# Statistics one tile ahead, a down product in two pieces and other room for two pools, in a four-layer forward and backward kernel

## Chip, cores, metric

One core of a Trainium2 chip. The metric is the device time of one execution in microseconds (us), as the median of several executions. TensorE is called PE, VectorE DVE, ScalarE ACT, GpSimd POOL; SyncE (SP) issues most of the transfers.

## The reference

Four residual layers, A, B, A, B, on x of 2048 x 512 in bf16, then the gradients for x and five weights. `setup_inputs` draws everything from a normal distribution times 0.05.

```python
def _A_ref(x, wqkv, wo):                    # linear attention, 32 heads of 16
    q, k, v = ...                           # (x @ wqkv) by heads
    phi = lambda t: jnp.where(t > 0, t + 1, jnp.exp(t)) + 1e-6
    pq, pk = phi(q), phi(k)
    kv = einsum("bhsd,bhse->bhde", pk, v);  z = einsum("bhsd->bhd", pk)
    num = einsum("bhqd,bhde->bhqe", pq, kv)
    den = einsum("bhqd,bhd->bhq", pq, z)[..., None] + 1e-6
    return (num / den).reshape(B, S, D) @ wo

def _B_ref(x, w_gate, w_up, w_down):        # GLU, 512 -> 1376 -> 512
    h = sigmoid(x @ w_gate) * (x @ w_up)
    return h @ w_down

x = x + _A_ref(_layernorm(x), A_wqkv, A_wo)
x = x + _B_ref(_layernorm(x), B_w_gate, B_w_up, B_w_down)
x = x + _A_ref(_layernorm(x), A_wqkv, A_wo)
x = x + _B_ref(_layernorm(x), B_w_gate, B_w_up, B_w_down)
# reference(): the value and its vjp with grad_out
```

## The kernel before, where the change touches it

The 2048 rows are 16 tiles of 128 (`NST`), four tiles make a block (`NB`), the 1376 hidden columns are 11 chunks (`NFC`). `after(k, x, y)` only fixes that x stands behind y; the compiler orders everything else by itself. First, the norm of layer 0: statistics on DVE, the inverse root of the variance on POOL, the scaling on DVE, then transposes on PE.

```python
if l == 0:
    src, rstd = narrow(k, st), k.rstd[l][:, st:st + 1]
    stats = k.small.tile([P, 6], F32, name="ln_stats")
    bn = nc.vector.bn_stats(stats[:], src)
    if 1 < st < 6:
        after(k, bn, self.applied[1 if st == 2 else st - 3])
    mv = k.small.tile([P, 2], F32, name="ln_mv")
    nc.vector.bn_aggr(mv[:], stats[:])
    mean = mv[:, 0:1]
    add = nc.gpsimd.tensor_scalar(rstd, mv[:, 1:2], EPS_LN, None, ALU.add)
    if 0 < st < 6:
        after(k, add, self.power)
    self.power = nc.gpsimd.tensor_tensor(rstd, rstd, k.neghalf[:, 0:1], ALU.pow)
    self.applied.append(nc.vector.tensor_scalar(self.h[b][:, j, :], src, mean, rstd, ALU.subtract, ALU.mult))
    # ... then four transposes on PE into T_ps
```

Between these stand the keys of the same tile: `k_ps` on PE, the exponential on ACT, two steps on DVE that end in `pk_t`, and then on PE the sum `E_ps` of h and pk.

```python
    nc.scalar.activation(pk, k_ps[:], ACT.Exp)
    nc.vector.tensor_scalar(pk, pk, 1.0, EPS, ALU.min, ALU.add)
    self.pks.append((pk, nc.vector.scalar_tensor_tensor(pk, k_ps[:], 1.0 + EPS, pk, ALU.add, ALU.max)))
```

Second, the first GLU. One chunk is eight matmuls (`g_ps`, `u_ps`), a tanh and a copy or two on ACT, one or two steps on DVE. The down product of a block is 44 matmuls, and it is issued at the start of the next block.

```python
def down(b):
    ys = [k.bank([P, D], F32, name="y_ps") for _ in range(NB)]
    for fcs in (range(NFC - 1), (NFC - 1,)):
        for j in range(NB):
            for fc in fcs:
                nc.tensor.matmul(ys[j][:], lhsT=hhs[b][fc][:, rows(j)], rhs=k.wd[:, fc, :], ...)
    for j in range(NB):
        add_x(k, b * NB + j, ys[j])

for b in range(NBLK):
    hhs[b] = []
    if b:
        down(b - 1)
    for fc in range(NFC):
        hh, sd = glu(k, ln.hT[b], fc, fc % 2 == 1, b == fc == 0)
        hhs[b].append(hh)
        # ... stores, and the next layer's norms
```

Third, the backward of that GLU, the inner gradient stage. Its two pools lie on the left side of SBUF, where the attention backward, which runs before and after it, has its own. At its end the attention backward wants `dqT_t` and `qn_l`, and a filling job (`Fill`, matmuls of another layer that plug PE's gaps) wants `hf_t`; all three are issued by SP, in order.

```python
def b_bwd(k, l):
    p_g = ctx.enter_context(k.tc.tile_pool(name=f"bb_g{l}", bufs=2))      # dhh_t
    p_dd = ctx.enter_context(k.tc.tile_pool(name=f"bb_dd{l}", bufs=5))    # dd_t
```

## Time and profile before

| | before |
|---|---|
| median of 4 executions (lowest to highest) | 1097.89 us (1096.7 to 1098.25) |
| span of the profiled one | 1095.3 us |
| PE busy | 1055.7 us, 96% |
| DVE, ACT, POOL busy | 51, 41, 28% |

First what DVE waited for most in the first 32 us (total us, times, longest us),

```profile
DVE h_t L295 <- POOL rstd L294: 4.5, 10, 0.9
```

then its timeline (start us, us busy, and in brackets the idle time before and what ended it),

```profile
7.81 0.17 DVE L289 BATCH_NORM_AGGREGATE ln_mv<-ln_stats 128x2 f32<-128x6 f32 x1
7.89 0.66 DVE L285 BATCH_NORM_STATS2 ln_stats<-x 128x6 f32<-128x512 bf16 x1
8.97 0.41 DVE L295 TENSOR_SCALAR h_t<-x,ln_mv,rstd 128x512 bf16<-128x512 bf16 x1 [0.42 <-POOL rstd L294]
```

and POOL's timeline for the same tile:

```profile
8.07 0.22 POOL L291 TENSOR_SCALAR rstd<-ln_mv 128x1 f32<-128x1 f32 x1 [1.81 <-DVE ln_mv L289]
8.37 0.57 POOL L294 TENSOR_TENSOR rstd<-rstd,neghalf 128x1 f32<-128x1 f32 x1
```

The aggregate starts at 7.81, POOL's add at 8.07, its power at 8.37, the scaling at 8.97: the round trip takes 1.16 us from the start of the aggregate.

### The profile page before, as it was taken

What the parts mean: (1) busy time and instruction counts of PE and PEld (TensorE: products, weight loads), DVE (VectorE), ACT (ScalarE), POOL (GpSimd) and SP (SyncE); (2) the same over time, 40 slices, a digit from 0 to 9 for tenths busy, and PEclk for the clock granted to TensorE, in tenths of its full rate; (3) what the DMA queues carried; (4) which work ended last, traced back from release to release, by engine and by line L of the source; (5) the groups of instructions that cost most, each with busy time, mean ns of one, the idle gap of its engine ahead of it and who ended that gap; (6) DMA issues with size and microseconds to landing.
All of it is one profiled execution on the core that took longest, in us unless ns stands there. A gap on an engine that the chain in (4) does not pass through costs nothing.

```text
span 1095.3 us, 15173 instructions
## 1 busy us (share of the span) xinstructions
PE 1055.7 (96%) x5355; PEld 493.4 (45%) x5448; DVE 554.0 (51%) x1029; ACT 444.0 (41%) x930; POOL 303.1 (28%) x410
## 2 busy tenths in 40 slices
PE   6989899999999999999999999998999999999998
PEld 3444344444444444444444444443444444465443
DVE  7686865669845454435776534557867200001110
ACT  4476766547845555543324533334326100000010
POOL 5333523203742525141622200003613200011110
PEclk9999999999999999999999999999999999999999
DMA  9997978789999989999997788769989998599991
GB/s 264 273 238 245 286 208 235 212 201 220 289 239 229 255 185 277 191 225 210 335 349 201 206 278 242 224 180 273 304 233 349 266 227 191 124 216 226 245 250 35
DMA packets 401869, 258.50 MB, mean 236 GB/s; under 512 B 308720, under 2 KB 371472, under 8 KB 400512
## 3 DMA queue, kind: packets, MB, share of 16 engines
q1 hardware_dynamic: 386608, 208.12, 77.9%
q0 software_dynamic: 15184, 49.39, 13.5%
q8 instruction: 43, 0.70, 0.3%
q14 instruction: 34, 0.28, 0.1%
HBM read 76.19 MB, written 106.79 MB: 167 GB/s over the span
## 4 chain that ended last, share of the span: by engine, by line
PE 66%; DMA 3%; DVE 2%; ACT 1%; issue 1%; POOL 1%; SPq 0%; ACTq 0%; DVEq 0%; POOLq 0%
PE dw_ps L1280 19%; PE dh_ps L840 7%; PE dh_ps L934 7%; PE dhh_ps L196 6%; PE dh_ps L1119 4%; PE y_ps L196 4%; PE dw_ps L1298 3%; PE g_ps L196 3%; PE u_ps L196 3%; PE dh_ps L1110 2%; PE fill_ps L250 2%; PE CT_ps L1038 2%; PE dq_ps L196 2%; PE dpk_ps L196 1%; DMA hf_t<-sv_hhT 1%
## 5 line engine op out<-in xcount | busy, mean ns | idle before, releaser
L1280 PE MATMUL dw_ps<-set_t,rows_t 128*128 128x512 bf16 (+1 forms) x1008 | 203.6, 362 | 0.8
L1280 PEld LDWEIGHTS <-rows_t 128*128 128x128 bf16 x1024 | 100.1, 98 | 103.7
L666 POOL TENSOR_TENSOR sd_t<-sd_t,hh_t 128x512 bf16<-128x512 bf16 x68 | 80.9, 1189 | 150.2 <-DVE hh_t L661 84.7
L1199 DVE CAST dw_new<-dw_ps 128x512 bf16<-128x512 f32 (+1 forms) x20 | 12.4, 654 | 184.1 <-PE dw_ps L1280 160.9
L1199 ACT CAST dw_new<-dw_ps 128x512 bf16<-128x512 f32 (+1 forms) x20 | 10.5, 561 | 225.7 <-PE dw_ps L1280 188.1
L904 ACT ACTIVATE t_sb<-dh_ps,rstd 128x512 f32<-128x512 f32 x64 | 43.5, 680 | 134.3 <-PE dh_ps L840 75.8
L196 PE MATMUL g_ps<-hT_t,wg 128*128 128x512 bf16 (+1 forms) x360 | 90.8, 375 | 1.2 <-DVE sd_t L663 0.6
L196 PE MATMUL u_ps<-hT_t,wu 128*128 128x512 bf16 (+1 forms) x360 | 90.7, 375 | 0.5 <-DVE hh_t L661 0.2
L196 PE MATMUL dhh_ps<-gT_t,wdT 128*128 128x512 bf16 x342 | 89.0, 379 | 1.2 <-ACT dhh_t L961 1.0
L934 PE MATMUL dh_ps<-wgT,dd_t 128*128 128x512 bf16 x174 | 66.0, 379 | 0.4
L934 PE MATMUL dh_ps<-wuT,dd_t 128*128 128x512 bf16 x169 | 64.1, 379 | 0.1
L661 DVE SCALAR_TENSOR_TENSOR hh_t<-sd_t,u_ps 128x512 bf16<-128x512 bf16 x88 | 59.4, 680 | 6.3 <-ACT sd_t L660 5.4
L1200 POOL DMA_DIRECT2D out_dram<-dw_new x36 | 19.3, 541 | 153.6 <-DVE dw_new L1199 150.2
L660 ACT ACTIVATE sd_t<-g_ps,onef 128x512 bf16<-128x512 f32 x88 | 60.5, 695 | 2.5
L963 DVE TENSOR_TENSOR dd_t<-dhh_t,sh_t 128x1024 bf16<-128x1024 bf16 x44 | 30.0, 691 | 58.9 <-ACT dhh_t L961 58.6
L659 ACT ACTIVATE g_ps<-g_ps 128x512 f32<-128x512 f32 x88 | 52.8, 606 | 7.7 <-PE g_ps L196 7.3
L749 DVE TENSOR_TENSOR sd_t<-dhh_t,sd_t 128x1024 bf16<-128x1024 bf16 x44 | 30.4, 691 | 48.7 <-POOL sd_t L666 45.8
L196 PEld LDWEIGHTS <-wu 128*128 128x128 bf16 x360 | 35.2, 98 | 41.5 <-issue 0.7
L196 PEld LDWEIGHTS <-wdT 128*128 128x128 bf16 x352 | 34.4, 98 | 42.6 <-issue 1.5
L196 PEld LDWEIGHTS <-wg 128*128 128x128 bf16 x360 | 34.5, 98 | 41.4 <-issue 1.8
L840 PEld LDWEIGHTS <-sd_t 128*128 128x128 bf16 x352 | 34.5, 98 | 41.5
L934 PEld LDWEIGHTS <-dd_t 128*128 128x128 bf16 x352 | 34.4, 98 | 41.6
(166 smaller groups left out, 1832.1 us busy)
## 6 DMA issues: line engine op xcount, KB each, us to landing
sv_sd<-sd_t SPq DMA_DIRECT2D x22, 512.0 KB, 3.7
sv_ddT<-dd_t SPq DMA_DIRECT2D x40, 256.0 KB, 5.0
sv_h<-h_t POOLq DMA_DIRECT2D x16, 512.0 KB, 5.3
sv_qr<-pe_t POOLq DMA_DIRECT2D x16, 512.0 KB, 4.9
sh_t<-sv_sd SPq DMA_DIRECT2D x8, 1024.0 KB, 6.8
rows_t<-sv_h SPq DMA_DIRECT2D x16, 512.0 KB, 8.5
sv_ddN<-nat_t SPq DMA_DIRECT2D x15, 512.0 KB, 4.4
set_t<-sv_ddN SPq DMA_DIRECT2D x12, 512.0 KB, 6.6
```

Source lines behind the costliest of these rows:

```text
L196: i = k.nc.tensor.matmul(out, lhsT=lhs(c), rhs=rhs(c), start=(c == 0), stop=(c == n - 1))
L659: nc.scalar.activation(g_ps[:], g_ps[:], ACT.Tanh, scale=-0.5)
L660: nc.scalar.activation(sd[:, 0, :], g_ps[:], ACT.Identity, bias=k.onef[:], scale=-1.0)
L661: nc.vector.scalar_tensor_tensor(hh[:], sd[:, 0, :], 0.5, u_ps[:], ALU.mult, ALU.mult)
L666: nc.gpsimd.tensor_tensor(sd[:, 1, :], sd[:, 1, :], hh[:], ALU.mult)
L749: k.last_mul = nc.vector.tensor_tensor(dd, dhh[:].unsqueeze(1).to_broadcast([P, 2, SB]), dd, ALU.mult)
L840: k.nc.tensor.matmul(dh[j][:], lhsT=dds[fc][:, a, rows(j)], rhs=(k.wuT, k.wgT)[a][:, fc, :], start=(a == fc == 0), stop=(a == 1 and fc == ...
L904: nc.scalar.activation(t_sb[:], dh_ps, ACT.Identity, scale=rstd, accum_out=c1[:])
L934: nc.tensor.matmul(acc[b][j][:], lhsT=dd[:, a, rows(j)], rhs=(k.wuT, k.wgT)[a][:, fc, :], start=(fc == 0 and a == 0), stop=(fc == NFC - 1 ...
L1119: nc.tensor.matmul(dh[j][:], lhsT=lhs(j, c), rhs=rhs(c), start=False, stop=stop and c == NDC - 1)
L1280: k.nc.tensor.matmul(ps[ic][:, 0:w], lhsT=h_m[:, ic * P:(ic + 1) * P], rhs=t_m, start=(m == 0), stop=(m == n - 1))
L1298: k.nc.tensor.matmul(p[0:r, :], lhsT=t[:, f:f + r], rhs=g_t, start=(i == 0 and st == 0), stop=(i == len(srcs) - 1 and st == NST - 1))
```

## The change

Three parts. The intent of the first is to take POOL's round trip off DVE's path by computing the statistics of tile t+1 before tile t is scaled. The second gives ACT and DVE two chunks of the GLU to work on while PE does the other half of the down product. The third keeps the inner gradient's tiles clear of the attention backward's room, so that its first loads need not wait.

```diff
         if l == 0:
-            (statistics, add, power and scaling of tile st, as above)
+            if st == 0:
+                self.stats(0)
+            if st + 1 < NST:
+                self.stats(st + 1)
+            mean, rstd = self.got.pop(st)
+            self.applied.append(nc.vector.tensor_scalar(self.h[b][:, j, :], narrow(k, st), mean, rstd, ALU.subtract, ALU.mult))
...
+    def stats(self, st):
+        bn = nc.vector.bn_stats(stats[:], narrow(k, st))
+        if 1 < st < 6:
+            after(k, bn, self.applied[st - 2])
+        (aggregate, add and power as above, without the order between tiles on POOL)
...
-    def down(b):
-        ys = [k.bank([P, D], F32, name="y_ps") for _ in range(NB)]
+    def down(b, js):
+        ys = {j: k.bank([P, D], F32, name="y_ps") for j in js}
         (and range(NB) becomes js in its loops)
...
         if b:
-            down(b - 1)
+            down(b - 1, range(2))
         for fc in range(NFC):
             hh, sd = glu(k, ln.hT[b], fc, fc % 2 == 1, b == fc == 0)
             hhs[b].append(hh)
+            if b and fc == 1:
+                down(b - 1, range(2, NB))
...
-    down(NBLK - 1)
+    down(NBLK - 1, range(NB))
...
-        p_g = ctx.enter_context(k.tc.tile_pool(name=f"bb_g{l}", bufs=2))
-        p_dd = ctx.enter_context(k.tc.tile_pool(name=f"bb_dd{l}", bufs=5))
+        p_g = ctx.enter_context(k.tc.tile_pool(name=f"bb_g{l}", bufs=2, side="right"))
+        p_dd = ctx.enter_context(k.tc.tile_pool(name=f"bb_dd{l}", bufs=5, side="right"))
```

More of the change, by code (lines that the diff above doesn't have):

```diff
@@ L267, in __init__ @@
         self.k, self.l = k, l
-        self.h, self.hT, self.done, self.applied = {}, {}, 0, []
+        self.h, self.hT, self.done, self.got, self.applied = {}, {}, 0, {}, []
     def need(self, st):
@@ L282, in one @@
         if l == 0:
-            src, rstd = narrow(k, st), k.rstd[l][:, st:st + 1]
-            stats = k.small.tile([P, 6], F32, name="ln_stats")
-            bn = nc.vector.bn_stats(stats[:], src)
-            if 1 < st < 6:
-                after(k, bn, self.applied[1 if st == 2 else st - 3])
-            mv = k.small.tile([P, 2], F32, name="ln_mv")
-            nc.vector.bn_aggr(mv[:], stats[:])
-            mean = mv[:, 0:1]
-            add = nc.gpsimd.tensor_scalar(rstd, mv[:, 1:2], EPS_LN, None, ALU.add)
-            if 0 < st < 6:
-                after(k, add, self.power)
-            self.power = nc.gpsimd.tensor_tensor(rstd, rstd, k.neghalf[:, 0:1], ALU.pow)
-            self.applied.append(nc.vector.tensor_scalar(self.h[b][:, j, :], src, mean, rstd, ALU.subtract, ALU.mult))
+            if st == 0:
[4 more added lines that the diff above has]
+            self.applied.append(nc.vector.tensor_scalar(self.h[b][:, j, :], narrow(k, st), mean, rstd, ALU.subtract, ALU.mult))
             if j % 2 == 0:
@@ L326, in one @@
                 store_turned(k, k.sv[l]["hT"][b], self.hT[b])
+    def stats(self, st):
+        k, nc = self.k, self.k.nc
+        rstd = k.rstd[self.l][:, st:st + 1]
+        stats = k.small.tile([P, 6], F32, name="ln_stats")
+        bn = nc.vector.bn_stats(stats[:], narrow(k, st))
+        if 1 < st < 6:
+            after(k, bn, self.applied[st - 2])
+        mv = k.small.tile([P, 2], F32, name="ln_mv")
+        nc.vector.bn_aggr(mv[:], stats[:])
+        nc.gpsimd.tensor_scalar(rstd, mv[:, 1:2], EPS_LN, None, ALU.add)
+        nc.gpsimd.tensor_tensor(rstd, rstd, k.neghalf[:, 0:1], ALU.pow)
+        self.got[st] = mv[:, 0:1], rstd
     def turn(self, j):
@@ L685, in store @@
             nc.sync.dma_start(out=sv["sd"][:, n - 1:n + 1], in_=sd[:].rearrange("p n a s -> p n (a s)"))
-    def down(b):
-        ys = [k.bank([P, D], F32, name="y_ps") for _ in range(NB)]
+    def down(b, js):
+        ys = {j: k.bank([P, D], F32, name="y_ps") for j in js}
         for fcs in (range(NFC - 1), (NFC - 1,)):
-            for j in range(NB):
+            for j in js:
                 for fc in fcs:
@@ L693, in down @@
                                      start=(fc == 0), stop=(fc == NFC - 1))
-        for j in range(NB):
+        for j in js:
             add_x(k, b * NB + j, ys[j])
```

## The prediction

> **What bounds the kernel now.** I read the page first. TensorE (PE) is busy 96% of the 1095.3 us span and every slice's granted clock is full, so only PE idle time, 1095.3 - 1055.7 = 39.6 us, can be won without removing matmuls, and the change removes none. Then I read what PE waited for, longest first. The columns are total us, times, longest us.
>
> ```profile
> PE 1055.7 (96%) x5355; PEld 493.4 (45%) x5448; DVE 554.0 (51%) x1029; ACT 444.0 (41%) x930; POOL 303.1 (28%) x410
> ...
> PE T_ps L299 <- DVE h_t L295: 6.6, 2, 5.9
> PE y_ps L692 <- DVE hh_t L661: 3.0, 2, 2.2
> PE fill_ps L250 <- DMA hf_t<-sv_hhT: 2.6, 1, 2.6
> ...
> PE T_ps L299 <- DVE pk_t L470: 1.9, 1, 1.9
> ...
> PE dhh_ps L196 <- ACT dhh_t L961: 1.0, 2, 0.6
> ```
>
> The changed places are the first norm (T_ps), the down product of the first GLU (y_ps L692), and the two ends of the inner gradient stage (dhh_ps, and fill_ps just after it). Third, busy time by stretch. After the stretch come its length and the busy us of PE, PE loads, DVE, ACT, POOL.
>
> ```profile
> 5.87:10.20 4.33, 3.50 (x16) 1.64 (x16) 3.41 (x9) 1.70 (x4) 1.72 (x5) 1.00 0.97 301
> 10.20:14.00 3.80, 1.92 (x9) 0.85 (x9) 3.07 (x10) 1.54 (x3) 3.46 (x9) 1.00 0.85 246
> ...
> 106.10:131.00 24.90, 23.69 (x137) 10.50 (x137) 21.13 (x40) 20.30 (x46) 10.16 (x14) 1.00 0.78 242
> 131.00:142.80 11.80, 9.57 (x44) 4.20 (x44) 4.44 (x7) 4.00 (x8) 3.98 (x5) 1.00 1.05 276
> ```
>
> From 5.87 to 30 us PE idles 4.6 us (my sum over six stretches: 0.83 + 1.88 + 0.75 + 0.27 + 0.43 + 0.45), though DVE is busy most of it. In the GLU, DVE (21.1 of 24.9 us) and ACT (20.3) run nearly full beside PE, then stand idle while PE does the 9.5 us down product. Last, the timelines: PE around a down product, and SyncE's queue and PE at the end of the inner gradient stage.
>
> ```profile
> 135.26 7.73 PE L692 MATMUL y_ps<-wd,hh_t 128*128 128x512 bf16 x35 [2.18 <-DVE hh_t L661]
> ...
> 733.07 2.93 SPq L830 DMA_DIRECT2D sv_ddT<-dd_t  x2
> 741.21 0.34 SPq L1028 DMA_DIRECT2D dqT_t<-sv_qr  x1
> 741.64 0.38 SPq L1033 DMA_DIRECT2D qn_l<-sv_qn  x1
> 742.08 4.92 SPq L238 DMA_TRANSPOSE hf_t<-sv_hhT  x1
> ...
> 750.58 0.39 PE L250 MATMUL fill_ps<-gf_t,hf_t 128*128 128x512 bf16 x1 [2.57 <-DMA hf_t<-sv_hhT]
> ```
>
> Between 736.00 and 741.21 SyncE issues nothing: the dqT_t load lands in memory that the dd tiles occupy, and PE reads the last dd until about 741.2. The DMA view of 735 to 741 us shows 0 GB/s from about 737.5 on.
>
> **What the Trainium skill says.** "Perfetto Trace Analysis", Optimization Strategy, says to find the gaps on the most contended engine and what blocks it; that is the reading above. The same page, DMA Instruction, HWDGE, puts the semaphore wait ahead of descriptor generation in the issuing sequencer, so a load that waits holds the loads behind it. The trace agrees: the qn_l and hf_t issues follow the blocked dqT_t issue within 0.9 us. "DMA: Bandwidth & Descriptors", Rules for kernel authors, advises to issue a DMA early and wait on it late; here the hf_t transpose took 8.46 us to land behind two 512 KB loads, where the fastest of the eleven took 4.5. "TensorE: Matmul & The Clock Gate", What's actually happening, says PE runs at half clock until it has been busy for about 3.4 us. The trace agrees in size (four k_ps matmuls take 1.89 us at 7.2 us, 1.03 us later); the change doesn't bring PE's first instruction forward, so I credit it nothing there.
>
> **Part 1, statistics one tile ahead.** Operations and their number stay: 16 times bn_stats 0.66 us, aggregate 0.17, add 0.22 and power 0.57 on POOL, scaling 0.41 on DVE. What goes is the round trip DVE, POOL, DVE between a tile's statistics and its scaling: DVE sat idle for it 10 times, 4.5 us in all. The first time (0.9 us, at 5.41) stays, since nothing can be ahead of tile 0, so PE still starts at 5.87. Tile 2's scaling, now at 8.97, can come at about 7.7: its bn_stats can start at 5.82, right after the first scaling, then 0.66 + 0.17 + 0.22 + 0.57 and hand-overs of about 0.2. The first pk_t, whose exponential is done at 9.7 but whose DVE steps stand behind later norm work until 13.95, should come 2 to 3 us sooner. That is the 1.9 us wait at 14.0; with the 0.7 us wait for h_t at 18.6 and some of the shorter ones I take 2.5 of the 4.6 us. It moves everything after it, as PE is 99% busy from 30 to 50 us.
>
> **Part 2, down product in two.** Three of the four products are split: 44 matmuls at 0.216 us = 9.5 us become 22 (4.75 us), two GLU chunks (16 matmuls, 3.45 us), 22 more. No work is added. ACT and DVE get two chunks 4.75 us sooner: on ACT two tanh (0.52 each, start to start), two sd_t copies (0.58) and one slope (0.57), 2.8 us; on DVE two hh_t and one sd_t at 0.60, 1.8 us. Both lie where these engines were idle (DVE 6.0 us before the sums at 105.7, 142.4 and 177.8). The lag with which hh_t trailed PE at the next block's end shrinks by up to 2.8 us, which covers the waits of 2.18 and 0.81 us there. PE's waits in the middle of these blocks (0.60, 0.55, 0.78, 0.21, 0.54) have the same lag behind them; I credit a third of them (0.9) and take back 0.9 for bank waits that the finer interleave can add. Sum: -3.0 us of 5.7.
>
> **Part 3, inner gradient tiles on the right.** The tiles no longer share room with what the attention backward keeps on the left, before or after. At the end, dqT_t and qn_l can go at about 736 into the idle queue; 1 MB at the 236 GB/s mean is 4.4 us, so they land as hf_t is issued. hf_t itself can't be issued before about 741.4, because its slot is free only when PE has finished the last matmul of the fill chunk before (741.0 + 0.4). From there 4.5 to 6 us puts it at 746 to 747.4, and PE wants it at 748.0. So the 2.57 us wait goes: -2.5. At the start the first dhh_t is written at 620.4, though its sums are ready at 616.7; behind it PE later waits 0.62 and 0.34 us. With free room ACT can take it earlier: -0.7, less than the whole because ACT's order there also hangs on a g_t cast.
>
> **Sum.** -2.5 - 3.0 - 2.5 - 0.7 = -8.7 us; 1097.86 - 8.7 = 1089.2. The compiler orders instructions anew, which in a kernel this dense tends to cost a little in untouched places; I allow 0.8 us and predict 1090.0.
>
> **Rivals.** (a) DVE is the limit of the first norm: per tile 0.66 + 0.17 + 0.41 for the norm and 0.26 + 0.67 for the keys is 2.17 us, against about 2.0 us of PE work. For it: DVE is 79 and 81% busy in the two stretches shown, where PE idles most. Against: norm work ends at 30 us, so DVE has slack afterwards to catch up. Then part 1 gives under 1 us: 1092. (b) hh_t of the block's last chunks is late whatever comes before, and because half a product now needs the last chunk after 20 matmuls (4.3 us) instead of 40 (8.6), the wait moves instead of vanishing. For it: at 135 PE needs chunk 9 after nine matmuls in both orders. Then part 2 gives nothing: 1093. (c) The hf_t load is hidden by nothing and lands as late as before, since other transfers move into its way (loads land in 7.4 us in the median for this tile): part 3 gives 1 us: 1092. (d) All three work in full, mid-block waits too: 4.0 + 5.0 + 3.5 = 12.5 us, 1085.3. (e) Reordering costs more than the gain: waits appear on a bank or a DMA; 1098 to 1101.
>
> **Range and chances.** Two rivals of (a) to (c) together give about 1095; (d) is 1085.3. I take 1085.5 to 1095.0. The idle time in all touched places is 4.6 + 5.7 + 3.6 = 13.9 us, 1.3% of the time, so faster by over 2% (22 us) is out of reach short of an effect that I don't see; slower by 2% would need a new stall of 22 us, which none of the moved waits can make.
>
> **What would show it.** Right: PE's busy time stays near 1055.7 and the span falls; the T_ps wait for pk_t and DVE's waits for rstd (4.5 us) shrink to about 1; the y_ps waits for hh_t vanish and the sums come in pairs; dqT_t is issued near 736 and the fill_ps wait is gone. Wrong: any of these waits at its old length, or a like sum of new PE waits on banks, rd_ps or a DMA. A time above 1095 would mean that reordering, which I can't read from the profile of before, decides.

## More of the kernel before

PE's records are not quite complete here (5355 matmuls of 5448, as the number of weight loads shows), so its busy time is read a little too low, and idle time is better read from the waits.

## The result, and the profile after

| | before | after |
|---|---|---|
| median of 4 executions | 1097.89 us | 1088.71 us (1087.64 to 1092.35) |
| ratio, 95% interval | | 0.9924 (0.99 to 0.9949) |
| span of the profiled one | 1095.3 us | 1086.5 us |
| idle PE from 97 to 210 us (stretch less busy time) | 6.0 us | 1.5 us |

A ratio here is the mean time of one kernel's fast executions over that of the other's of the same rounds, so it is not quite the ratio of the medians quoted beside it.

The changed kernel is 9.2 us faster by the medians. The busy line of the page after the change:

```profile
PE 1061.0 (98%) x5448; PEld 494.9 (46%) x5448; DVE 551.7 (51%) x1029; ACT 445.0 (41%) x930; POOL 305.0 (28%) x410
```

PE's waits over the whole span, longest first, with total us, times and longest us (line numbers are those of the changed kernel, so T_ps moved from L299 to L292, y_ps from L692 to L698):

```profile
PE T_ps L292 <- DVE h_t L288: 6.0, 2, 5.8
PE fill_ps L250 <- DMA hf_t<-sv_hhT: 1.7, 1, 1.7
PE T_ps L292 <- DVE pk_t L476: 1.2, 1, 1.2
PE g_ps L196 <- DMA hT_t<-h_t: 1.0, 2, 0.7
PE dhh_ps L196 <- ACT dhh_t L969: 0.6, 2, 0.3
```

The 3.0 us of y_ps waiting for hh_t are gone. The fill_ps wait fell from 2.6 to 1.7 us only, the pk_t wait from 1.9 to 1.2, and g_ps has a wait for the hT_t transposes that was not there. PE's busy time is 1061.0 us, not near 1055.7; the two can't be compared, as all 5448 matmuls are in this record and only 5355 in that of before. The 39.6 us of idle PE that the prediction starts from are too many for the same reason. DVE in the first norm now, first its longest wait in the first 32 us, then its timeline:

```profile
DVE h_t L288 <- POOL rstd L332: 3.6, 7, 1.0
```

```profile
7.25 0.17 DVE L330 BATCH_NORM_AGGREGATE ln_mv<-ln_stats 128x2 f32<-128x6 f32 x1
7.34 0.66 DVE L326 BATCH_NORM_STATS2 ln_stats<-x 128x6 f32<-128x512 bf16 x1
8.42 0.41 DVE L288 TENSOR_SCALAR h_t<-x,ln_mv,rstd 128x512 bf16<-128x512 bf16 x1 [0.42 <-POOL rstd L332]
```

It is the same picture as before, 0.55 us earlier: aggregate, one bn_stats, 0.42 us idle, scaling. "One tile ahead" in the source put one bn_stats between a tile's statistics and its scaling, and the compiler's order had one there already. PE at the first split down product:

```profile
129.60 4.97 PE L698 MATMUL y_ps<-wd,hh_t 128*128 128x512 bf16 x22
134.91 1.04 PE L196 MATMUL g_ps<-hT_t,wg 128*128 128x512 bf16 x4 [0.34 <-DMA hT_t<-h_t]
...
138.82 4.91 PE L698 MATMUL y_ps<-wd,hh_t 128*128 128x512 bf16 x22
```

Two times 22 matmuls, no wait for hh_t, and a short one for the next block's transposes, which the chunks now need 4.75 us sooner. Last, SP's timeline before and at the end of the inner gradient stage, and PE's just after it:

```profile
608.56 1.20 SPq L1041 DMA_DIRECT2D qn_l<-sv_qn  x1
...
726.68 2.93 SPq L838 DMA_DIRECT2D sv_ddT<-dd_t  x2
734.82 0.34 SPq L1036 DMA_DIRECT2D dqT_t<-sv_qr  x1
735.25 3.77 SPq L238 DMA_TRANSPOSE hf_t<-sv_hhT  x1
```

```profile
742.71 0.82 PE L250 MATMUL fill_ps<-gf_t,hf_t 128*128 128x512 bf16 x3 [1.66 <-DMA hf_t<-sv_hhT]
```

The qn_l load moved to 608.56, some 130 us forward, but dqT_t did not: SP still stands still for 5.2 us after the last dd store (729.61 to 734.82), and hf_t follows behind it. In the compiled program's placement, which I read outside the traces, the four dqT_t tiles take bytes 152608 to 168992 of a partition, and the dd tiles, now on the right, 166880 to 177120. They still share 2112 bytes; `no_overlap` below tests that.

### The profile page after: what moved, and what is told of

It is laid out like the page before. It is cut to its first block, busy times and chain, and to the rows that moved or that the text cites. A ratio compares the mean times of both kernels' runs of the same rounds, so it can differ in the third digit from the quotient of the medians.

```text
span 1086.5 us, 15262 instructions
## 1 busy us (share of the span) xinstructions
PE 1061.0 (98%) x5448; PEld 494.9 (46%) x5448; DVE 551.7 (51%) x1029; ACT 445.0 (41%) x930; POOL 305.0 (28%) x410
## 4 chain that ended last, share of the span: by engine, by line
PE 68%; DMA 2%; ACT 2%; DVE 1%; issue 1%; POOL 0%; SPq 0%; ACTq 0%; DVEq 0%; POOLq 0%
PE dw_ps L1288 19%; PE dh_ps L848 7%; PE dh_ps L942 7%; PE dhh_ps L196 6%; PE dh_ps L1127 5%; PE y_ps L196 4%; PE dw_ps L1306 3%; PE g_ps L196 3%; PE u_ps L196 3%; PE dh_ps L1118 3%; PE dpk_ps L196 2%; PE CT_ps L1046 2%; PE fill_ps L250 2%; PE dq_ps L196 2%; DMA hf_t<-sv_hhT 1%
## 5 line engine op out<-in xcount | busy, mean ns | idle before, releaser
L942 PE MATMUL dh_ps<-wuT,dd_t 128*128 128x512 bf16 x176 | 66.7, 379 | 0.0
```

The costliest lines, as they stand in the source:

```text
L942: nc.tensor.matmul(acc[b][j][:], lhsT=dd[:, a, rows(j)], rhs=(k.wuT, k.wgT)[a][:, fc, :], start=(fc == 0 and a == 0), stop=(fc == NFC - 1 ...
```

## The experiments

Two profiled executions of the same code can differ by more than a part of the change is worth, so I read each part from its own stage: the time from the first PE matmul of the stage to the first of the next one. All in us, one profiled execution each.

| kernel | parts | first norm and keys: T_ps to first down | GLU: first down to third layer's q_ps | inner gradient to attention backward: dhh_ps to dkvT_ps | time, median | ratio to before, 95% |
|---|---|---|---|---|---|---|
| before | none | 90.77 | 121.77 | 169.86 | 1097.89 | |
| p1_alone | 1 | 90.68 | 121.81 | 170.65 | 1097.97 | 0.998 (0.9943 to 1.0016) |
| p2_alone | 2 | 91.43 | 116.80 | 170.10 | 1094.27 | 0.9952 (0.9913 to 0.999) |
| p3_alone | 3 | 91.43 | 123.46 | 168.65 | 1096.74 | 0.9973 (0.9934 to 1.0011) |
| p23 | 2, 3 | 91.53 | 116.92 | 168.70 | 1090.62 | 0.9931 (0.9901 to 0.996) |
| after | 1, 2, 3 | 90.90 | 117.02 | 168.40 | 1088.71 | 0.9924 (0.99 to 0.9949) |
| after_again | 1, 2, 3 | 91.65 | 116.74 | 168.74 | 1090.30 | 0.9923 (0.9896 to 0.995) |
| no_overlap | and room freed | 90.96 | 117.54 | 169.76 | 1092.83 | 0.9932 (0.9897 to 0.9966) |
| no_overlap_2 | and loads ordered | 91.18 | 117.01 | 167.29 | 1088.61 | 0.9906 (0.9878 to 0.9934) |
| ahead2_best | and two tiles ahead | 89.91 | 116.65 | 167.40 | 1087.88 | 0.9901 (0.9874 to 0.9929) |
| split31 | 1, 2 as 3:1, 3 | 91.11 | 120.03 | 168.01 | 1091.70 | 0.9931 (0.9905 to 0.9956) |

The kernel before was run 11 times beside each set of four: medians 1099.2, 1097.95 and 1097.91. p1_alone, p2_alone, p3_alone and no_overlap ran in the first set; no_overlap_2 in the second, with three kernels told of below; p23, after_again, ahead2_best and split31 in the third. The rows before and after are the first comparison of the two. The first two sets ran on one chip, the third on another.

The traces' record of the granted clock has to be read beside this table. The granted clock is the share of its full clock that PE gets. In some executions it falls to half for one stretch of 3.41 us; `prof` with `--windows` shows it as 0.50, as here in after_again:

```profile
15.30:18.60 3.30, 3.08 (x18) 1.65 (x17) 3.14 (x9) 0.42 (x2) 2.04 (x5) 0.50 1.01 384
```

p2_alone, p3_alone, p23, after_again and no_overlap have such a stretch between 13 and 19 us; before, p1_alone, after, no_overlap_2, ahead2_best and split31 have none there. In the column of the first norm that is worth comparing: with the same code there, before took 90.77 us without the stretch and p2_alone, p3_alone and p23 91.43 to 91.53 with it. p3_alone has two more, from 137.1 and from 331.7 us, and split31 one in its GLU, told of below. (Up to the record's first event, at 9.9 to 16.3 us in these kernels, `--windows` prints 1.00. That is no measurement: four k_ps matmuls took 1.89 us there and 1.03 later.)

### Each part alone

`p1_alone`, `p2_alone` and `p3_alone` are the kernel before with one part of the diff above each.

> Part 1 alone. Theory: its gain is nearly nothing, 0 to -1 us, because the compiler fills the freed DVE time with statistics of later tiles that stand before the first pk_t, so pk_t comes only 0.3 us sooner, and PE stays at half clock until about 16 us; the down product then starts at 96.5 to 96.8 us as in the kernel before (96.6). Rival, the prediction: -2.5 us, down product at about 94. If 1.3 us more show up after 210 us with the GLU unchanged, the gains of untouched places come from part 1's new order.

> Part 2 alone. Theory: -4.7 us by the end of the last down product (it ends 4.7 us sooner than in the kernel before), as in the trace of the whole change; whole time -4.5 to -6. Rival, the prediction's sum: -3. Rival b: nothing, because the late hh_t only moves the wait.

> Part 3 alone. Theory: -1.3 us of it at both ends of the inner gradient stage (0.4 where dhh_ps waits, 0.9 of the 2.57 us where fill_ps waits for hf_t), because dqT_t still waits for the last dd tile and only qn_l goes early; up to 1.4 us more after 755 us if the earlier qn_l also moves later loads. Whole time -1 to -3. Rival, the prediction: -3.2 at the two ends, fill_ps wait gone.

Measured: part 1 alone left its stage at 90.68 us and DVE's wait for rstd at 3.6 us, 7 times, as in the full change. (Its down product started at 97.19 us and not near 96.6, because PE's first transpose came 0.6 us later.) Part 2 alone took its stage from 121.8 to 116.8 us. Part 2 also took all 5.7 us of PE's waits in that stage with it, at the ends and in mid-block, and brought 0.8 us for hT_t and 0.5 for hh_t. Part 3 alone took 1.2 us off its stage, 168.65 against 169.86. The profiled execution of p3_alone was also the slowest of its six (1102.76 us, the others 1095.07 to 1097.4); what was slow in it lies in other stages (the half clock from 137.1 us among it), so only its last stage is read. By the medians (before 1099.2 in these rounds) the parts are 1.2, 4.9 and 2.5 us, which adds up to 8.6; the intervals of parts 1 and 3 include no effect, so for these two the stages decide.

### What holds the first norm

Here I had two theories. PE is cold in its first microseconds (four k_ps matmuls take 1.89 us at 7.1 us), which delays the exponentials and so the DVE steps of pk_t; or DVE has no room for pk_t sooner, whatever PE does. `warm_before` and `warm_after` put matmuls on a zeroed tile in front, in a bank whose first real product starts anew, so that PE is warm when the transposes come.

```diff
+WARM = 40
...
+    k.warm = consts.tile([P, P], BF16, name="warm")
+    nc.vector.memset(k.warm[:], 0.0)
...
+        if l == 0:
+            for _ in range(WARM):
+                nc.tensor.matmul(E_ps[0][:, 0:P], lhsT=k.warm[:], rhs=k.warm[:], start=True, stop=True)
         ln.need(1 if l == 0 else 0)
```

> The kernel before with 40 matmuls of 128x128 zeros that nobody reads, before PE's first transpose. Theory: PE leaves its half clock before 5.9 us instead of at 12 to 16 us; the four k_ps matmuls of tile 0 take about 1.0 us instead of 1.9, and the down product starts 1 to 2 us sooner than at 96.6. Rival: the first norm is bound by DVE, and PE only waits longer for pk_t: under 0.5 us.

> The changed kernel with the same 40 matmuls. Theory: part 1's gain was eaten by the half clock, which lasted to about 16 us there; with a warm PE the changed kernel gains more from the warming than the kernel before does, and the down product starts 1.5 to 2.5 us sooner than in the warm kernel before. Rival: DVE order, not the clock, takes the gain; then the two warm kernels start the down product within 0.7 us of each other.

The ratios were 1.0002 (0.9974 to 1.003; 1099.48 us) and 0.9917 (0.9884 to 0.995; 1090.71 us), and the stage took 91.39 and 91.42 us: no gain. PE's timeline of warm_after shows why:

```profile
6.97 1.04 PE L199 MATMUL k_ps<-wkvo,hT_t 128*128 128x512 bf16 x4 [0.68 <-ACT hT_t L299]
...
13.47 0.38 PE L295 MATMUL T_ps<-ident,h_t 128*128 128x128 bf16 x4 [2.90 <-DVE pk_t L479]
```

The keys are ready sooner (1.04 us instead of 1.89), and PE waits 2.90 us for pk_t instead of 1.2. The clock theory fell: what PE gained it gave back waiting for DVE. Both warm executions have a stretch of half clock afterwards (15.0 to 18.4 and 14.8 to 18.2 us), so their like are p2_alone, p3_alone and p23 (91.43 to 91.53) and after_again (91.65): no gain either way. (The extra tile moves other tiles' places in SBUF, and both have more half clock between 745 and 756 us; only the first stage is read here.)

`pkfirst_warm` then forces DVE to do the first two pk_t before more statistics.

```diff
         if 1 < st < 6:
             after(k, bn, self.applied[st - 2])
+        if st in (4, 6):
+            after(k, bn, k.pk0[st // 2 - 2])     # k.pk0: the last DVE step of each pk_t
```

> As warm_after, with the statistics of tile 4 ordered behind the first pk_t and those of tile 6 behind the second. Theory of the DVE order: the first pk_t, finished at 13.6 us in the changed kernel, is finished near 10.6; E_ps starts near 12 instead of 14.1, and the down product starts 1 to 2 us sooner than in warm_after. Rival: DVE is short by its total work up to 30 us, and the time saved at 14 us is lost again as waits for pk_t or h_t before 30 us: within 0.5 us of warm_after.

The step that ends the first pk_t moved from 12.73 to 10.32 us as expected, but the stage grew from 91.42 to 93.39 us: 2 us worse, which neither theory had (1091.01 us in all, against 1090.71). Its chief new wait of PE:

```profile
PE E_ps L522 <- DVE pk_t L481: 3.8, 5, 1.8
```

With the keys ahead, the norms behind them came late, then their keys, and DVE's wait for rstd rose from 3.6 to 4.6 us. PE's waits for h_t, pk_t and hT_t in this stage grew by about 1.4 us over warm_after's. The half clock fell elsewhere too, from 21.6 to 25.0 us, so not all of the 2 us need be DVE's order. I read the waits so: what is taken for one tile is missing for the next. Between 5 and 31 us DVE was busy for 21.8 of 26 us before the change and 22.2 after it.

`p23` and `after_again` are the change without part 1 and with it, side by side.

> Parts 2 and 3 without part 1. If part 1 is worth nothing (the theory that VectorE's own work bounds the first norm): the same as the changed kernel of these rounds within 0.1% (1.1 us). If part 1 gives the 2.5 us that was predicted: 0.23% slower than the changed kernel. From the trace: first transpose to first down product 90.7 to 91.5 us, against 90.2 to 91.2 with part 1.

> The changed kernel once more, in the same rounds as the other three. All theories: 0.9895 to 0.9935 of the kernel before, span 1086 to 1091 us; from the first transpose to the first down product 90.2 to 91.2 us; from the first down product to the first query of the third layer 116.8 to 117.6 us.

1090.62 and 1090.30 us; their first stages took 91.53 and 91.65 us. Part 1 as written gains nothing that can be measured: over all profiled kernels that differ in it alone as to the first stage, the means are 91.29 us without it (before, p2_alone, p3_alone, p23) and 91.08 with it (p1_alone, after, after_again, no_overlap, no_overlap_2, split31), 0.2 us where single executions of the same code lie 0.75 us apart. Compared by the clock it is no different: with the half-clock stretch 91.43 to 91.53 without part 1, 90.96 and 91.65 with it; without the stretch 90.77, and 90.68 to 91.18 with part 1.

### Two tiles ahead

If one bn_stats of 0.60 us between is too little, more must stand between. A first version that only emitted the statistics of tile t+2 was ordered by the compiler exactly as the changed kernel, so it was not run. `ahead2_best` forces it, on top of the freed room and the ordered loads told of below.

```diff
             if st == 0:
                 self.stats(0)
-            if st + 1 < NST:
-                self.stats(st + 1)
+                self.stats(1)
             mean, rstd = self.got.pop(st)
             self.applied.append(nc.vector.tensor_scalar(...))
+            if 0 < st < NST - 1:
+                after(k, self.applied[-1], self.ag[st + 1])   # ag: the aggregates
+            if st + 2 < NST:
+                self.stats(st + 2)
```

> Statistics two tiles ahead, forced by an order edge (scaling of tile t after the aggregate of tile t+1), on top of the version with freed room and ordered loads. Between the aggregate of a tile and its scaling now stand one scaling (0.41 us), one bn_stats (0.60) and one aggregate (0.17), 1.2 us, more than the 1.1 us of the round trip: VectorE's waits for rstd after the first one fall from 2.7 us to under 0.8 (all theories). Theory (VectorE's work and its order bound the first norm): the second and later pk_t come up to 2 us sooner, the first one not; first transpose to first down product changes by less than 0.7 us. Rival (the round trip alone bounds it): 2 us or more shorter, 88.9 us or below. The rest of the kernel as in the second run of the version without overlap: dq to dkv stretch 39.5 to 40.3 us, time 0.990 of before, or 0.988 by the rival.

DVE's wait for rstd in the first 32 us, and its timeline at the place shown above:

```profile
DVE h_t L287 <- POOL rstd L335: 1.9, 3, 1.0
```

```profile
8.08 0.18 DVE L333 BATCH_NORM_AGGREGATE ln_mv<-ln_stats 128x2 f32<-128x6 f32 x1
8.21 0.41 DVE L287 TENSOR_SCALAR h_t<-x,ln_mv,rstd 128x512 bf16<-128x512 bf16 x1
```

The gaps of 0.42 us are gone, seven waits became three, and 0.95 of the 1.9 us left is tile 0's, which nothing can cover. The other 0.95 is a little over the 0.8 expected. The step that ends the second pk_t starts at 13.85 us instead of 15.92, that of the first at 12.35 instead of 12.95. The stage took 89.91 us, the shortest of all, in one profiled execution without half clock: 1.1 us under the mean of the four with part 1 that had none either (90.97). That is more than the theory's 0.7 and less than the rival's 2. Both seem to have a share: the edit that covers the round trip is worth about 1 us. It also changes DVE's order, so the two are not separated. The time was 1087.88 us against 1090.30 for after_again in the same rounds; of that, about 1.3 us (167.40 against 168.74) comes from the last stage.

### How much lead the GLU needs

`split31` splits the down product three to one, which halves the lead that ACT and DVE get.

```diff
-            down(b - 1, range(2))
+            down(b - 1, range(3))
...
-                down(b - 1, range(2, NB))
+                down(b - 1, range(3, NB))
```

> The changed kernel with the down product split three to one instead of two to two: three sums, two chunks, one sum. ScalarE and VectorE get their first two chunks 2.4 us sooner than before the change instead of 4.75 us. Theory (the lead that these engines gain is what removed the waits, and it is more than enough; the only new wait is for hT_t, because the chunks start before its transposes have landed): the two g_ps waits for hT_t (0.3 and 0.7 us) vanish, at most 1 us of waits for hh_t or sd_t comes back, and the stretch from the first down product to the third layer's first query stays at 116.5 to 117.7 us. Rival (the lead is needed in full): waits for hh_t, sd_t and pe_t come back to about half of before's 5.7 us, and the stretch is 118.5 to 120 us.

The waits for hT_t vanished, as the theory said. But the stage took 120.03 us, the upper end of the rival's range. PE's timeline at the end of the second block,

```profile
132.07 0.43 PE L698 MATMUL y_ps<-wd,hh_t 128*128 128x512 bf16 x1 [2.02 <-ACT sd_t L671]
```

and the busy times of the stretch behind it (start and end, length, then busy us of PE, PE loads, DVE, ACT, POOL, and the granted clock):

```profile
132.07:142.00 9.93, 9.71 (x38) 4.20 (x39) 4.72 (x11) 2.94 (x6) 3.10 (x3) 0.83 0.87 287
132.30:135.60 3.30, 3.08 (x8) 1.21 (x8) 3.13 (x6) 2.65 (x5) 1.72 (x2) 0.50 1.03 281
```

The lag came back at the block's end. L671 is the copy by which ACT reads g_ps, and y_ps has no data from it, so this wait can only be for the bank of PSUM (the memory that matmuls write to). The same copy ended at 129.56 us in the changed kernel and at 132.02 here, 2.5 us later, which is the lead that was given up. And the granted clock of the stretch behind it was 0.83, which is half clock for 3.41 us and full clock for the rest: 31 matmuls took 8.32 us, against 7.29 for 32 a block later. So some 2.2 us of waits and 1.3 us of clock, less 1.0 us of hT_t waits saved. In mid-block 0.8 us of waits for hh_t stood, against 0.5 in the changed kernel; there, half the lead was nearly enough. "More than enough" was wrong: at the block's end a lead of 2.4 us was not enough in this execution and one of 4.75 us was. The clock's part was in neither expectation. The times show less of it: 1091.70 us against 1090.30 for after_again in the same rounds, with ratios whose intervals overlap.

### The room of dqT_t

`no_overlap` takes the 2112 shared bytes away: a pool that needs one buffer gets one, and another 14 instead of 16.

```diff
-        k.p_part = mpool("wd_part", 2)
+        k.p_part = mpool("wd_part", 1)
...
-            k.sums[st // 2] = k.small.tile([P, 2], F32, name="x_sum", bufs=NST)
+            k.sums[st // 2] = k.small.tile([P, 2], F32, name="x_sum", bufs=NST - 2)
```

> The whole change, and 2112 bytes of SBUF per partition freed on the left (one wd_part buffer and two x_sum buffers less), so that the room of the four dqT_t tiles no longer reaches into that of the dd tiles. Theory: dqT_t's load waits in the changed kernel only because those rooms overlap by 2112 bytes; without it dqT_t and qn_l are issued long before 735 us, hf_t is alone in the queue and lands within about 5 us, the fill_ps wait of 1.66 us goes: 1 to 1.7 us faster than the changed kernel, -10 to -11 against before. Rival: hf_t takes 7 us whatever is ahead of it, because its own transpose is slow; then the wait stays at about 1.5 us and the time is the changed kernel's, -9.

SP's timeline:

```profile
612.01 0.47 SPq L1036 DMA_DIRECT2D dqT_t<-sv_qr  x1
...
737.18 1.76 SPq L1266 DMA_TRANSPOSE set_t<-sv_ddT  x1
739.03 3.06 SPq L238 DMA_TRANSPOSE hf_t<-sv_hhT  x1
```

The dqT_t load now goes at 612.01 instead of 734.82, so the overlap is shown to be what held it. But the stage got no shorter (169.76 us), as the compiler had put a set_t transpose, needed later, in front of hf_t; the fill_ps wait was 2.1 us, and the 1 to 1.7 us of gain that I expected did not come. `no_overlap_2` orders these loads behind the last hf_t.

```diff
+        self.ld = self.k.nc.sync.dma_start_transpose(out=t[:, :, 0:w], in_=...)       # hf_t
...
+        ld = k.nc.sync.dma_start...(out=t[:], ...)                                   # set_t
+        after(k, ld, k.fill.ld)
```

> As no_overlap, where the load of a set_t tile of the last stage moved in front of hf_t; here the set_t loads are ordered behind the last hf_t load. Theory: with nothing queued between 732 and 735 us hf_t is issued within 0.4 us of the last read of its slot and lands within 5 us, fill_ps waits under 0.5 us instead of 2.1, the stretch from the first dq_ps to the first dkvT_ps of the outer layer shrinks from 41.3 to about 39.5 us. Rival: the transpose takes 6.5 to 7.5 us whatever is ahead, and the wait stays above 1.2 us.

```profile
737.39 1.89 SPq L238 DMA_TRANSPOSE hf_t<-sv_hhT  x1
```

Nothing stands before hf_t in SP's timeline now, the fill_ps wait is gone, and the stage took 167.29 us (167.40 in ahead2_best, which has the same edit): 2.9 us under the mean of the three kernels without part 3 (170.20), where part 3 as written gives 1.7 (168.50 over after, after_again, p3_alone, p23, split31). Why part 3 as written gives that much is not shown. The fill_ps wait is 1.0 to 1.8 us in these five (in p23 the profile puts it down to ACT), against 2.6 in the kernels without part 3, and the early qn_l looks like the cause; but in warm_after and pkfirst_warm qn_l goes as early, and the wait is 2.8 and 2.7 us.

## Why the prediction came out right, and where it did not

The time was 1088.71 us for 1090.0 predicted, well inside the range. That it came so close is luck: parts 1 and 3 gave less than their terms, part 2 gave more, the cost of reordering did not appear, and 2.4 of the 9.2 us belong to no part. Of the signs that the prediction named for being right, two failed: DVE's waits for rstd did not shrink to about 1 us, and the fill_ps wait did not go. (Its starting value, 1097.86, is one execution's; the median is 1097.89.)

| term of the sum | predicted | measured by its stage |
|---|---|---|
| part 1 | -2.5 | -0.2, not resolved |
| part 2 | -3.0 | -4.9 (from 121.8, the mean of before and p1_alone, to 116.9, that of after, after_again, p2_alone and p23) |
| part 3, end and start | -2.5 and -0.7 | -1.7 together |
| reordering elsewhere | +0.8 | not seen |

**Part 1.** The step that failed is "What goes is the round trip DVE, POOL, DVE between a tile's statistics and its scaling". It did not go. The round trip is 1.1 to 1.2 us, what stands in it is one bn_stats of 0.60, and DVE's rstd waits fell from 4.5 us to 3.6, not "to about 1". "Tile 2's scaling can come at about 7.7" failed twice: x of tile 2 landed only at 6.33 (DVE waited 0.55 us for it), and the trip took its time from there, to 8.42. The first pk_t came 0.3 us sooner instead of 2 to 3, as the compiler filled DVE's freed time with statistics of later tiles; 19 steps of the norm stand in front of it before the change, 18 after. Rival (a), that DVE limits the first norm, was the better account: it said under 1 us.

**Part 2.** The mechanism was right and a size was off: "I credit a third of them (0.9)" for the waits in mid-block, and 0.9 taken back for new ones. All 2.7 us of mid-block waits went along with the 3.0 us at the ends, as rival (d) had it, and the new waits were 1.0 us for hT_t and 0.5 for hh_t. Waits alone give -5.7 + 1.5 = -4.2; the two profiled executions differ by 4.75 us in this stage. A wait on a transfer was among the dangers of rival (e), but not in this sum.

**Part 3.** The step that failed is "At the end, dqT_t and qn_l can go at about 736 into the idle queue". "The tiles no longer share room" was taken from the sides of the pools and not from addresses. qn_l went, dqT_t did not. The rest of that step held when it was tried: with the room truly free and nothing else in front, the fill_ps wait of 2.6 us was gone. At the start ACT's first dhh_t came 4.4 us after the stage's first matmul instead of 4.8, but 5.3 us in after_again, which is the same code: the 0.7 us predicted there are not seen.

**What is left.** The measured terms add up to 6.8 us, the medians differ by 9.2 in the first comparison and 7.6 in the repeat (1097.91 to 1090.30). The two profiled spans differ by 8.8, of which 1.3 is a stage that no part touches (before took 49.64 us from the first dpk_ps product of the last attention backward to dw_ps, with a wait of 1.1 us for the haT_l load; all 13 other profiled kernels 48.35, without that wait) and 1.3 more lies between the third layer and the inner gradient, where kernels with the same code there range from 395.3 to 398.4 us (but for the slow execution of p3_alone, 403.3). I take this for variation between executions; that it is nothing else is not shown. Neither of the two profiled executions has half clock between 17 us and the end of that stage, so the clock is not the reason here.

## What to carry to other kernels

"One ahead" in the source says little: read how long the round trip is and what the compiler already puts into it, and force the order if more is needed. Splitting a long PE-only product around work that feeds the other engines paid more than the waits at its own ends suggested, because those engines' lag was behind the later waits too; at the block's end half the lead was not enough. Moving a pool to the other side frees a load only if the addresses no longer meet; look at where the tiles lie, and at which transfer steps into the gap. Before comparing one stage of two executions, look whether the clock was at half in one of them. The version with parts 1 and 3 mended (ahead2_best, 1087.88 us) beat both kernels; against the change itself that is 0.2%, close to what executions of one kernel vary by.

## What the Trainium skill lacked or had wrong

- "TensorE: Matmul & The Clock Gate", What's actually happening, has PE fall to half clock after at least one idle window of about 3.4 us. The length of the stretch agrees: 3.41 us at half clock in split31 (132.26 to 135.67) and in after_again (15.27 to 18.69). The condition, if idle means without any matmul, does not: PE was busy for 1.39 and 1.63 us of the 3.41 us before these two, and the longest gap in split31 was 2.02 us. What the condition is stays open: in the kernel before, a gap of 2.18 us and 3.41 us with PE busy for 1.54 (from 11.57) were both followed by full clock.
- "GPSIMD Engine Reference", Elementwise — side-by-side cycle accounting, has a model per element and an add of 2048 columns, and no total for the fixed part on GpSimd. What mattered here was the fixed cost of an operation on one column, 0.22 us for the add and 0.57 us for the power, and the round trip from VectorE and back, about 1.16 us from the start of the aggregate.
- No page gives the time of the batch-norm statistics: 0.60 to 0.66 us for 512 columns, 0.17 us for the aggregate.
- No page warns that a load can be held by a small overlap of its room with that of a tile still in use, here 2112 bytes of 16384: the dqT_t load was issued at 734.82 us with the overlap and at 612.01 without.
